# A written order for the sync queue, with stores between the last loads, and a new order of the steps in a retention and token-mixing kernel

## The chip, the cores and the metric

The kernel runs on one core of a Trainium2 chip. The time is the device time of the core in microseconds; the number compared is the median over runs. The profile is that of one execution, and its span runs from the first to the last instruction that the profiler recorded.

## What is computed

Two layers follow each other. The first is a retention recurrence over 768 tokens for 4 batches and 8 heads of 64:

```python
gamma = 1.0 - 2.0 ** (-5.0 - np.arange(H, dtype=np.float32))
for t in range(S):
    state = gamma[None, :, None, None] * state + np.einsum('bhd,bhe->bhde', k[:, :, t], v[:, :, t])
    y[:, :, t] = scale * np.einsum('bhd,bhde->bhe', q[:, :, t], state)
```

Its output is laid out as x, 768 tokens by 512 features in each batch. The second layer mixes tokens with weights that it makes from x, applies a relu, and projects:

```python
wq = x @ w_q
wk = x @ w_k
W_tok = scale * np.einsum('bsd,btd->bst', wq, wk)
mixed = np.einsum('bst,btd->bsd', W_tok, x)
return (np.maximum(mixed, 0.0) @ w_out).astype(np.float32)
```

Inputs and output are float32. q, k and v have 6.3 MB each, the output 6.3 MB.

## The kernel before

**Tiles.** The tokens of a batch are cut into three pairs of chunks of 128 tokens, twelve pairs in all (0 to 11). Of each pair, k, q and v are loaded whole, 512 KB each. The kernel computes in bf16 into PSUM, which is used as eight numbered banks.

**Steps.** Every piece of work is a named step with a pair, mostly a half or chunk, an engine (A for ScalarE, V for VectorE, P for GpSimd) and a PSUM bank. The list `ORDER` writes all steps down in one sequence, and a loop at the end of the kernel issues them as listed; there is no scheduler behind it, and each engine runs its own steps in the sequence of the list. For a pair p the steps are:
- `ck.p.c`, `cq.p`, `cv.p.c`: cast k and q from the loaded tile to bf16; scale and cast v (ck and cv are two instructions each). In the profile of before a cast on ScalarE is under L133, one on VectorE or GpSimd under L134, cv under L307.
- `trk`, `trq`: eight transposes each on TensorE (L335, L350); `ekT`, `eqT` copy the results out of PSUM.
- `sc.p.half`: products of q and k (L370); `eat`: masks them (L382). `st.p.c`: adds to the running state (L424); `es` copies it out. `in` and `ia`: the two parts of y, from the state (L410) and from the masked products (L444). `ex`: scales y into x (L458).
- `xt`, `exT`: transposes x (L474). `wqk`: x times w_q and w_k (L488), with `ewq` and `ew` copying out; `tw` and `ewt`: the transposed wq (L514). `zm.b`, `ez`: wk-transposed times x, summed over the three pairs of a batch (L536). `mx`: z times wq (L556); `r`: the relu (L571, L573).
- `pj.p.j`: the projection with w_out, four matmuls for each half j (L578); `eo.p.j`: copies the half into the output tile.
- `W` and `WO` cast the weights. `fill.n` issues n matmuls on zeros (L283), whose results nobody reads.

**Buffers.** Loaded tiles share a pool of 18 buffers: a load may be issued when the tile 18 places ahead of it has been cast. Bf16 k, q and v have three buffers each, transposed k and q two, the relu two, output tiles ten. A bank is written again only after its last reader.

**The sync queue.** SyncE issues all transfers but half of the first k, in program order; each instruction waits for its own semaphores, and those behind it wait too. `LOADS` gives the sequence of the loads (k, q, v with their pair, `w` for w_q and w_k, `o` for w_out). `more_loads` issues them as far as the buffers allow, and is called again when a tile has been cast. Stores are collected in `eo`: a pair is stored when both halves are evicted, pair 11 by halves. They are issued only when the list of loads is empty, in the sequence of their evictions:

```python
        if p == NG - 1:
            stores.append((p, j))
        elif outs[p] == 2:
            stores.append((p, None))
        if not queue:
            while stores:
                store(*stores.pop(0))
```

Loads are under L152 in the profile, stores under L609 (pair) and L611 (half).

Of the kernel before, what the change touches and what calls it, by code (L numbers as in the profile page):

```python
# [13 lines left out]


ORDER = """
ck.0.1:A cq.0.1:V ck.0.0:P fill.20@6 trk.0@6 cq.0.0:A ekT.0:V fill.1@0 trq.0@0 eqT.0:A fill.4@0
sc.0.1@0 ck.1.0:P sc.0.0@2 cv.0.0:V ck.1.1:A cq.1:A cv.0.1:P ck.2.1:P st.0.0 eat.0.1:V cv.1.1:P
fill.3@6 trk.1@6 fill.3@0 trq.1@0 eat.0.0:V ekT.1:A cv.2.0:P ia.0.1@2 ck.3.1:P es.0.0:V cv.1.0:V
st.0.1 in.0.1@2 ia.0.0@2 eqT.1:A sc.1.1@0 ck.2.0:A cv.2.1:P sc.1.0@4 ex.0:V es.0.1:A cq.2:A  # L20
fill.1@6 xt.0@6 st.1.0 eat.1.1:V es.1.0:A in.1.0@2 eat.1.0:V trk.2@0 ekT.2:V trq.2@1 exT.0:A
eqT.2:V ck.3.0:A ia.1.1@2 in.1.1@2 ia.1.0@2 fill.1@0 sc.2.0@0 st.1.1 ex.1:V es.1.1:A fill.2@6
xt.1@6 cv.3.0:P in.2.0@2 sc.2.1@4 st.2.0 eat.2.0:V trk.3@0 cq.3:A eat.2.1:V trq.3@1 es.2.0:A
in.2.1@2 exT.1:A eqT.3:A ia.2.1@2 ia.2.0@2 ekT.3:V ex.2:V fill.2@0 sc.3.0@0 sc.3.1@4 ck.4.0:P
eat.3.0:V eat.3.1:V cv.3.1:P st.3.0 W:A cv.4.0:P wqk.0@6 ck.4.1:A es.3.0:A xt.2@2 cq.4:A trk.4@3
wqk.1@0 ew.1:A ewq.1:A in.3.1@4 ewq.0:A trq.4@1 ia.3.1@4 cv.4.1:P ia.3.0@4 eqT.4:A ck.5.0:P
exT.2:V st.3.1 es.3.1:A ew.0:V wqk.2@6 ekT.4:V sc.4.1@0 tw.0@3 st.4.0 ew.2:A ewq.2:A ex.3:V
ewt.0:A eat.4.1:V cv.5.0:P sc.4.0@4 tw.1@6 tw.2@3 eat.4.0:V zm.0@2 es.4.0:A WO:P xt.3@0 ez.0:V
cq.5:A exT.3:V ewt.2:A trq.5@1 ck.5.1:A ewt.1:V ia.4.1@4 in.4.1@4 in.4.0@4 st.4.1 ia.4.0@4
wqk.3@6 es.4.1:V ck.6.0:P eqT.5:A ewq.3:A mx.2@2 trk.5@1 ex.4:V st.5.0 r.2:A xt.4@0 tw.3@2  # L30
ew.3:A ewt.3:A mx.1@4 es.5.0:A ekT.5:V r.1:A cv.5.1:P sc.5.0@2 exT.4:V eat.5.0:V sc.5.1@0
ck.6.1:A eat.5.1:V wqk.4@6 pj.2.0@4 ew.4:A pj.2.1@5 cv.6.0:P trk.6@0 cq.6:A eo.2.1:V ekT.6:V
ck.7.1:P eo.2.0:A trq.6@1 mx.0@4 eqT.6:V ewq.4:A r.0:A in.5.1@2 ck.7.0:A in.5.0@2 ia.5.1@2
ia.5.0@2 pj.1.0@6 sc.6.0@4 eo.1.0:A cv.6.1:P sc.6.1@0 ex.5:V cq.7:A st.6.0 xt.5@2 eat.6.0:V
exT.5:A cv.7.0:P pj.0.1@6 ck.8.0:P trk.7@4 eat.6.1:V cv.7.1:P es.6.0:V trq.7@5 wqk.5@2 ia.6.0@0
ekT.7:A ia.6.1@0 eqT.7:V ewq.5:V in.6.1@0 st.6.1 sc.7.1@4 ew.5:A eo.0.1:A ex.6:V sc.7.0@2
eat.7.1:V zm.1@6 es.6.1:A ck.8.1:A ez.1:A st.7.0 tw.5@0 cq.8:A eat.7.0:V ewt.5:A pj.1.1@1
trk.8@6 trq.8@4 eo.1.1:A ekT.8:V tw.4@5 es.7.0:A eqT.8:V ewt.4:A in.7.0@2 mx.5@0 in.7.1@2
ia.7.1@2 cv.8.0:P ia.7.0@2 r.5:A pj.0.0@6 ck.9.0:A cq.9:P ex.7:V eo.0.0:A st.7.1 sc.8.0@0
sc.8.1@4 es.7.1:V mx.4@2 st.8.0 eat.8.0:V pj.5.0@6 ck.9.1:A eat.8.1:V es.8.0:A xt.6@0 eo.5.0:A  # L40
cv.8.1:P xt.7@1 r.4:A trq.9@6 ck.10.0:A exT.6:V ck.10.1:P trk.9@4 ia.8.0@2 exT.7:V cv.9.0:P
ekT.9:A eqT.9:V cv.9.1:P wqk.6@0 ew.6:A wqk.7@1 trk.10@6 ia.8.1@2 in.8.1@2 in.8.0@2 ewq.6:V
ewq.7:A ew.7:V ekT.10:V ex.8:V sc.9.1@4 eat.9.1:V sc.9.0@0 cq.10:A st.9.0 ck.11.1:P pj.4.0@6
pj.5.1@2 es.9.0:A eat.9.0:V xt.8@3 eo.4.0:A trq.10@6 exT.8:V st.9.1 eo.5.1:A mx.3@4 eqT.10:V
ck.11.0:A in.9.1@0 cq.11:P ia.9.0@0 tw.6@2 r.3:A ia.9.1@0 ewt.6:A wqk.8@3 ex.9:V trk.11@6
trq.11@2 sc.10.1@4 cv.10.0:P ew.8:A es.9.1:A ewq.8:A tw.8@3 pj.3.0@0 ekT.11:V xt.9@6 eat.10.1:V
eqT.11:A ewt.8:A tw.7@1 sc.10.0@4 exT.9:V sc.11.1@2 eo.3.0:A ewt.7:A cv.10.1:P st.10.0 es.10.0:A
zm.2@1 st.10.1 es.10.1:A cv.11.0:P pj.4.1@6 ez.2:A st.11.0 eat.11.1:V eat.10.0:V sc.11.0@0
mx.8@2 es.11.0:A in.10.1@4 cv.11.1:P eat.11.0:V eo.4.1:A in.10.0@4 ia.10.1@4 ia.10.0@4 pj.3.1@6
ia.11.1@0 r.8:A in.11.1@0 ex.10:V mx.7@2 in.11.0@0 mx.6@4 eo.3.1:A ia.11.0@0 pj.8.0@6 ex.11:V  # L50
r.7:A wqk.9@2 xt.10@3 ewq.9:A ew.9:V pj.7.1@0 xt.11@2 exT.10:V wqk.10@3 ewq.10:A eo.8.0:V
exT.11:V eo.7.1:V pj.8.1@6 wqk.11@2 ew.10:V r.6:V ewq.11:A tw.9@3 pj.7.0@0 eo.8.1:V tw.11@1
ew.11:A ewt.11:A zm.3@2 eo.7.0:A ez.3:V pj.6.0@6 ewt.9:V tw.10@3 mx.9@0 mx.11@4 eo.6.0:A
ewt.10:V r.9:A mx.10@2 pj.6.1@6 pj.9.1@0 r.10:V pj.9.0@1 eo.6.1:A r.11:A pj.10.1@6 eo.10.1:A
pj.10.0@2 pj.11.1@6 eo.9.0:V pj.11.0@1 eo.11.1:A eo.10.0:V eo.11.0:A eo.9.1:V
""".split()


LOADS = "q0 v0 k1 q1 v1 k2 q2 v2 k3 q3 v3 w k4 q4 v4 k5 q5 v5 o k6 q6 v6 k7 q7 v7 k8 q8 v8 k9 q9 v9 k10 q10 v10 k11 q11 v11".split()

STAGES = 18
OBUFS = 10
# [3 lines left out]
def kernel(  # L66
# [15 lines left out]
    nc = tc.nc  # L82
# [7 lines left out]
    NG = B * NP  # L90
# [36 lines left out]
    pairs = [dict() for _ in range(NG)]  # L127
# [3 lines left out]
    def copy(e, out, in_):  # L131
        if e == "A":
            return nc.scalar.copy(out=out, in_=in_)  # L133
        return ENGINES[e].tensor_copy(out=out, in_=in_)  # L134
# [10 lines left out]
    def load(name, p, half=None, eng=None):  # L145
        src = {"k": k, "q": q, "v": v}[name]
        b, cp = divmod(p, NP)
        st = pairs[p]
        if name + "_st" not in st:
            st[name + "_st"] = stage_pool.tile([128, 2, HP, 2, D], FP32, name=name + "_st", tag="st")  # L150
        xs = slice(0, 2) if half is None else slice(half, half + 1)
        dma = (eng or nc.sync).dma_start(  # L152
            out=st[name + "_st"][:, xs].rearrange("g x hp j d -> g (x hp) (j d)"),
            in_=src[b, xs.start * HP : xs.stop * HP, cp * 2 * C : (cp + 1) * 2 * C, :].rearrange(
                "h (g j) d -> g h (j d)", j=2
            ),
        )
    def load_token(token):
        if token == "w":
            nc.sync.dma_start(out=wq_stage, in_=moe_w_q.rearrange("(a p) h -> p a h", p=128))  # L160
            nc.sync.dma_start(out=wk_stage, in_=moe_w_k.rearrange("(a p) h -> p a h", p=128))
        elif token == "o":
            for a in range(NDM):
                nc.sync.dma_start(
                    out=wout_stage[:, a], in_=moe_w_out[128 * a : 128 * a + 128, :], max_dma_last_dim=512
                )
        else:
            name, _, half = token[1:].partition("/")
            load(token[0], int(name), int(half) if half else None)

    load("k", 0, 0, nc.scalar)
    load("k", 0, 1, nc.sync)

    queue = list(LOADS)
    staged = ["k0"]
    cast = set()


    def more_loads():
        while queue:  # L180
            token, _, half = queue[0].partition("/")
            if token not in "wo" and token not in staged:
                n = len(staged)
                if n >= STAGES and staged[n - STAGES] not in cast:
                    return
                staged.append(token)
            load_token(queue.pop(0))
# [3 lines left out]
    def release(token, n):  # L191
        parts[token] = parts.get(token, 0) + 1
        if parts[token] == n:
            cast.add(token)
            more_loads()

    more_loads()


# [384 lines left out]
            )  # L584
        st["o_ps", j] = bank32(b)

    outs = {}

    def eo(e, b, p, j):
        st = pairs[p]  # L590
        if "o" not in st:
            st["o"] = ost_pool.tile([128, 2, DM], FP32, name="o_st")
        copy(e, st["o"][:, j], st["o_ps", j])
        outs[p] = outs.get(p, 0) + 1
        if p == NG - 1:
            stores.append((p, j))
        elif outs[p] == 2:
            stores.append((p, None))
        if not queue:
            while stores:  # L600
                store(*stores.pop(0))

    stores = []

    def store(p, j):
        b, cp = divmod(p, NP)
        dst = out[b, cp * 2 * C : (cp + 1) * 2 * C, :].rearrange("(g j) m -> g j m", j=2)
        if j is None:
            nc.sync.dma_start(out=dst, in_=pairs[p]["o"], max_dma_last_dim=512)  # L609
        else:  # L610
            nc.sync.dma_start(out=dst[:, j], in_=pairs[p]["o"][:, j], max_dma_last_dim=512)  # L611

    steps = dict(
        ck=ck, cq=cq, cv=cv, trk=trk, ekT=ekT, trq=trq, eqT=eqT, sc=sc, eat=eat, st=state,
        es=es, ia=ia, **{"in": inter}, ex=ex, xt=xt, exT=exT, wqk=wqk, ewq=ewq, ew=ew, tw=tw, ewt=ewt, zm=zm, ez=ez, mx=mx, r=r,
        pj=pj, eo=eo,
    )

    for token in ORDER:
        token, _, b = token.partition("@")  # L620
        token, _, e = token.partition(":")
# [38 lines left out]
```

## Time and profile before

| | |
|---|---|
| median of 9 runs | 103.4 us (102.22 to 104.27) |
| the profiled execution | 103.23 us, span 101.3 us |
| granted TensorE clock, mean | 0.979 |
| TensorE, VectorE busy | 87.1 us, 72.9 us |
| ScalarE, GpSimd busy | 71.7 us, 67.1 us |
| read from HBM, written to it | 20.19 MB, 6.29 MB |
| last load issued, landed | 62.59 us, 68.99 us |
| last store issued, landed | 96.27 us, 100.47 us |

Busy times overlap, and busy TensorE is not TensorE at its peak, since matmuls are pipelined. In the lines of the profile PE is TensorE, DVE VectorE, ACT ScalarE, POOL GpSimd, and SPq the queue of SyncE. A timeline line has start, duration, engine, line of the code, operation and tiles; a line of the chain has start, duration and what the last instruction was waiting for at that time. A row by stretch has the stretch and its length, then each engine's busy time with its instructions in brackets, then the granted clock, the busy share of the 16 transfer engines and what they moved.

### The profile page before, as it was taken

How to read it: one execution, taken by the hardware profiler on the slowest of the kernel's cores; microseconds unless marked ns; L12 is line 12 of the kernel's file. 1: busy time of each engine (PE TensorE's matmuls, PEld its weight loads, DVE VectorE, ACT ScalarE, POOL GpSimd, SP SyncE). 2: the span in 40 equal slices, each digit the busy share in tenths (PEclk: the TensorE clock that was granted, in tenths of full speed). 3: DMA queues.
4: the chain of work that ended last, by engine and by line, in shares of the span. 5: the costliest groups of instructions: out<-in, count | busy, mean ns of one | idle time of the engine just before them, and what ended most of it. 6: DMA issues, size and time to landing. Idle time of an engine off the chain costs nothing.

```text
span 101.3 us, 3245 instructions
## 1 busy us (share of the span) xinstructions
PE 87.1 (86%) x1341; PEld 59.7 (59%) x1341; DVE 72.9 (72%) x108; ACT 71.7 (71%) x125; POOL 67.1 (66%) x86
## 2 busy tenths in 40 slices
PE   5995996999688799989998989999999999999300
PEld 1343674767576587566875669659667776544100
DVE  3017599998949958879999795699898689445200
ACT  4275798789697599889899999959947614645400
POOL 6542969999899997999999999999998000000000
PEclk9999999999999999999999999999999999999965
DMA  1999999999999999999999999999921930686395
GB/s 24 292 347 347 347 347 344 298 267 265 289 283 324 262 287 304 313 280 330 328 320 317 300 277 329 340 335 334 347 89 32 298 91 0 190 244 190 106 346 169
DMA packets 53134, 26.68 MB, mean 263 GB/s; under 512 B 1920, under 2 KB 53120, under 8 KB 53120
## 3 DMA queue, kind: packets, MB, share of 16 engines
q1 hardware_dynamic: 52592, 26.22, 87.4%
q10 hardware_dynamic: 528, 0.26, 0.9%
q8 instruction: 10, 0.16, 0.6%
q14 instruction: 4, 0.03, 0.1%
HBM read 20.19 MB, written 6.29 MB: 261 GB/s over the span
## 4 chain that ended last, share of the span: by engine, by line
PE 38%; POOL 16%; DMA 13%; ACT 9%; SPq 7%; DVE 6%; issue 4%; ACTq 0%; DVEq 0%; POOLq 0%
PE banks L578 15%; POOL vs L307 12%; DMA q_st<-in_q_dram 7%; SPq L152 7%; DMA k_st<-in_k_dram 6%; POOL ks L134 4%; DVE at_sb L382 3%; PE banks L444 3%; ACT ks L133 3%; PE banks L488 3%; PE banks L350 3%; PE banks L370 3%; PE banks L474 2%; PE banks L556 2%; PE banks L424 2%
## 5 line engine op out<-in xcount | busy, mean ns | idle before, releaser
L307 POOL TENSOR_TENSOR vs<-v_st,fv 64x512 bf16<-64x512 f32 x44 | 45.9, 1044 | 3.0 <-DMA v_st<-in_v_dram 0.2
L382 DVE TENSOR_TENSOR at_sb<-banks,cmask 128x1024 bf16<-128x1024 f32 x24 | 28.4, 1217 | 2.3 <-POOL ks L134 1.2
L578 PE MATMUL banks<-wout_sb,relu 128*128 128x512 bf16 x96 | 23.6, 379 | 0.2
L133 ACT CAST ks<-k_st 64x512 bf16<-64x512 f32 x26 | 16.0, 616 | 4.0 <-DMA k_st<-in_k_dram 3.7
L134 POOL CAST ks<-k_st 64x512 bf16<-64x512 f32 x22 | 14.2, 645 | 6.2 <-DMA k_st<-in_k_dram 4.9
L458 DVE TENSOR_TENSOR x_nat<-banks,fy 128x1024 bf16<-128x1024 f32 x12 | 14.7, 1221 | 2.4 <-PE banks L444 2.1
L578 PEld LDWEIGHTS <-relu 128*128 128x128 bf16 x96 | 8.5, 97 | 8.7 <-issue 1.0
L283 PE MATMUL banks<-warm 128*128 128x512 bf16 x37 | 11.3, 438 | 2.4 <-DVE warm L202 1.3
L133 ACT COPY o_st<-banks 128x512 f32<-128x512 f32 x17 | 10.0, 586 | 4.3 <-PE banks L578 4.1
L571 ACT ACTIVATE relu<-banks 128x1024 bf16<-128x1024 f32 x10 | 10.3, 1031 | 1.7 <-PE banks L578 1.2
L133 ACT CAST qs<-q_st 128x1024 bf16<-128x1024 f32 (+1 forms) x10 | 10.1, 1006 | 1.8 <-DMA q_st<-in_q_dram 1.6
L444 PE MATMUL banks<-vs,at_sb 128*128 128x64 bf16 x192 | 8.8, 194 | 0.2 <-POOL vs L307 0.2
L370 PE MATMUL banks<-qT,kT 64*128 64x128 bf16 x192 | 8.3, 218 | 0.6 <-DVE wqn L134 0.2
L350 PE MATMUL banks<-identity,qs 128*128 128x128 bf16 x96 | 7.3, 220 | 1.7 <-ACT qs L133 1.4
L133 ACT CAST s_sb<-banks 128x256 bf16<-128x256 f32 x16 | 6.0, 377 | 3.2 <-PE banks L424 3.0
L474 PE MATMUL banks<-identity,x_nat 128*128 128x128 bf16 x96 | 7.2, 220 | 0.9 <-DVE x_nat L458 0.9
L444 PEld LDWEIGHTS <-at_sb 128*128 128x128 bf16 x192 | 7.2, 98 | 1.1 <-issue 0.5
L335 PE MATMUL banks<-identity,ks 128*128 128x128 bf16 x96 | 7.4, 220 | 0.4 <-POOL ks L134 0.4
L370 PEld LDWEIGHTS <-kT 64*128 64x128 bf16 x192 | 5.9, 94 | 3.1 <-issue 2.4
L350 PEld LDWEIGHTS <-qs 128*128 128x128 bf16 x96 | 5.9, 98 | 2.9 <-ACT qs L133 2.1
L283 PEld LDWEIGHTS <-warm 128*128 128x128 bf16 x37 | 3.7, 110 | 6.6 <-issue 3.6
L474 PEld LDWEIGHTS <-x_nat 128*128 128x128 bf16 x96 | 5.8, 98 | 2.9 <-DVE x_nat L458 1.7
(59 smaller groups left out, 120.6 us busy)
## 6 DMA issues: line engine op xcount, KB each, us to landing
q_st<-in_q_dram SPq DMA_DIRECT2D x12, 512.0 KB, 6.3
v_st<-in_v_dram SPq DMA_DIRECT2D x12, 512.0 KB, 6.5
k_st<-in_k_dram SPq DMA_DIRECT2D x11, 512.0 KB, 6.5
out_dram<-o_st SPq DMA_DIRECT2D x11, 512.0 KB, 4.2
wout_stage<-in_moe_w_out_dram SPq DMA_DIRECT2D x4, 256.0 KB, 5.0
out_dram<-o_st SPq DMA_DIRECT2D x2, 256.0 KB, 2.9
k_st<-in_k_dram ACTq DMA_DIRECT2D x1, 256.0 KB, 4.2
k_st<-in_k_dram SPq DMA_DIRECT2D x1, 256.0 KB, 3.8
```

What stands on the lines that cost most here:

```text
L133: return nc.scalar.copy(out=out, in_=in_)
L134: return ENGINES[e].tensor_copy(out=out, in_=in_)
L283: nc.tensor.matmul(out=bank32(b), lhsT=warm[:, 0:128], rhs=warm, start=True, stop=True)
L307: ENGINES[e].tensor_tensor(out=st["vs"][rows(j), c].rearrange("p hp x d -> p x hp d"), in0=st["v_st"][rows(c), :, :, j], in1=fv[rows(c), p ...
L350: nc.tensor.transpose(ps[:, hp, :, j, :], st["qs"][:, hp, j].rearrange("p x d -> p (x d)"), identity,)
L370: nc.tensor.matmul(out=ps[:, x, hi, c, :], lhsT=st["kT"][rows(x), hp, c, :], rhs=st["qT"][rows(x), hp, c, :], start=(hi == 0 and c == 0), ...
L382: ENGINES[e].tensor_tensor(out=st["at", half].rearrange("p x hi c t -> p (x hi c) t"), in0=st["at_ps", half].rearrange("p (n t) -> p n t", ...
L444: nc.tensor.matmul(out=y[:, x, c, hp, :], lhsT=st["at", half][:, x, hi, c, :], rhs=st["vs"][:, c, hp, x, :], start=first(p, x), stop=False ...
L458: nc.vector.tensor_tensor(out=st["x"].rearrange("p x c i n -> p (x c i n)").rearrange("p (m d) -> p m d", d=D), in0=st["y_ps"].rearrange(" ...
L474: nc.tensor.transpose(ps[:, a, c, :], st["x"][:, a // 2, c, a % 2, :], identity)
L571: nc.scalar.activation(out=dst, in_=st["mx_ps"], func=ACT.Relu)
L578: nc.tensor.matmul(out=bank32(b), lhsT=st["relu"][:, a, j, :], rhs=wout_sb[:, a, :], start=(a == 0), stop=(a == NDM - 1),)
```

## The change

The list of the sync queue now holds stores as well, `s` with the pair, or with pair and half. `more_loads` stops at a store until its halves have been evicted, issues it, and goes on. The evictions call `more_loads` where they kept a list of their own. Up to q10 the loads keep their sequence; s0 then comes ahead of v10, s1 behind k11, s2 behind q11, and the remaining stores behind v11.

`ORDER` is written anew as a whole: the same steps (apart from six `fill` steps with 28 matmuls in place of nine with 37), in another sequence, partly on other engines and banks. Steps per engine that differ:

| step | before (A, V, P) | after (A, V, P) |
|---|---|---|
| ck | 13, 0, 11 | 15, 2, 7 |
| cq | 10, 1, 2 | 8, 1, 4 |
| cv | 0, 2, 22 | 0, 1, 23 |
| ekT | 3, 9, 0 | 5, 7, 0 |
| exT | 3, 9, 0 | 6, 6, 0 |
| es | 16, 4, 0 | 13, 7, 0 |
| ewq | 10, 2, 0 | 8, 4, 0 |
| ewt | 9, 3, 0 | 6, 6, 0 |
| r | 10, 2, 0 | 9, 3, 0 |

GpSimd's list in the new order, from pair 5 on: cv.5.0, cv.5.1, WO, cq.6, cv.6.0, cv.6.1, ck.7.1, cv.7.0, cv.7.1, cv.8.1, cv.8.0, ck.9.1, cq.9, ck.10.0, cq.10, cv.9.0, cv.9.1, ck.11.0, cq.11, cv.10.0, cv.10.1, cv.11.0, cv.11.1. Before, WO stood ahead of ck.6.0 and cv.5.1, and the end of the list was cq.9, cv.8.1, ck.10.1, cv.9.0, cv.9.1, ck.11.1, cq.11, cv.10.0, cv.10.1, cv.11.0, cv.11.1.

The core of the diff, with the last rows of both orders:

```diff
-ew.11:A ewt.11:A zm.3@2 eo.7.0:A ez.3:V pj.6.0@6 ewt.9:V tw.10@3 mx.9@0 mx.11@4 eo.6.0:A
-ewt.10:V r.9:A mx.10@2 pj.6.1@6 pj.9.1@0 r.10:V pj.9.0@1 eo.6.1:A r.11:A pj.10.1@6 eo.10.1:A
-pj.10.0@2 pj.11.1@6 eo.9.0:V pj.11.0@1 eo.11.1:A eo.10.0:V eo.11.0:A eo.9.1:V
...
+ewq.10:V eo.7.1:A wqk.11@3 ew.11:A tw.9@6 pj.7.0@2 ewq.11:A tw.10@3 ewt.10:V zm.3@4 ewt.9:A
+pj.8.0@6 ez.3:V tw.11@3 eo.7.0:A eo.8.0:A mx.10@4 mx.9@0 ewt.11:V mx.11@2 pj.8.1@6 r.10:A
+pj.10.1@4 r.11:V pj.10.0@5 eo.10.1:V pj.11.1@2 pj.11.0@4 eo.8.1:A eo.10.0:A r.9:V pj.9.0@6
+eo.9.0:A pj.9.1@5 eo.11.0:V eo.9.1:A eo.11.1:V
...
-LOADS = "q0 v0 k1 q1 v1 k2 q2 v2 k3 q3 v3 w k4 q4 v4 k5 q5 v5 o k6 q6 v6 k7 q7 v7 k8 q8 v8 k9 q9 v9 k10 q10 v10 k11 q11 v11".split()
+LOADS = """
+q0 v0 k1 q1 v1 k2 q2 v2 k3 q3 v3 w k4 q4 v4 k5 q5 v5 o k6 q6 v6 k7 q7 v7 k8 q8 v8 k9 q9 v9 k10
+q10 s0 v10 k11 s1 q11 s2 v11 s4 s3 s5 s6 s7 s8 s10 s11/0 s11/1 s9
+""".split()
...
     def more_loads():
         while queue:
-            token, _, half = queue[0].partition("/")
-            if token not in "wo" and token not in staged:
+            token = queue[0]
+            if token[0] == "s":
+                if not stored(token[1:]):
+                    return
+                queue.pop(0)
+                continue
+            if token not in "wo":
...
         copy(e, st["o"][:, j], st["o_ps", j])
-        outs[p] = outs.get(p, 0) + 1
-        if p == NG - 1:
-            stores.append((p, j))
-        elif outs[p] == 2:
-            stores.append((p, None))
-        if not queue:
-            while stores:
-                store(*stores.pop(0))
+        evicted.add((p, j))
+        more_loads()
...
+    def stored(name):
+        p, _, j = name.partition("/")
+        p, js = int(p), [int(j)] if j else [0, 1]
+        if not all((p, i) in evicted for i in js):
+            return False
         b, cp = divmod(p, NP)
         dst = out[b, cp * 2 * C : (cp + 1) * 2 * C, :].rearrange("(g j) m -> g j m", j=2)
-        if j is None:
-            nc.sync.dma_start(out=dst, in_=pairs[p]["o"], max_dma_last_dim=512)
-        else:
-            nc.sync.dma_start(out=dst[:, j], in_=pairs[p]["o"][:, j], max_dma_last_dim=512)
+        src = pairs[p]["o"]
+        if j:
+            dst, src = dst[:, int(j)], src[:, int(j)]
+        nc.sync.dma_start(out=dst, in_=src, max_dma_last_dim=512)
+        return True
```

## Prediction

> **What bounds the kernel now.** I read the slices of the page first, then busy time by stretch, then the chain that ended last, then the timelines of POOL and of the sync queue.
>
> ```profile
> PE   5995996999688799989998989999999999999300
> DMA  1999999999999999999999999999921930686395
> GB/s 24 292 347 347 347 347 344 298 267 265 289 283 324 262 287 304 313 280 330 328 320 317 300 277 329 340 335 334 347 89 32 298 91 0 190 244 190 106 346 169
> ```
>
> Transfers are busy to about 73 us, nearly idle afterwards, and full again in the next to last slice (346 GB/s), when PE has already stopped.
>
> ```profile
> core 0: us, PE busy (x) PEld busy (x) DVE busy (x) ACT busy (x) POOL busy (x), PEclk, DMA share, GB/s
> 8.00:44.00 36.00, 30.89 (x553) 22.86 (x552) 30.96 (x37) 29.61 (x50) 30.76 (x33) 1.00 1.04 305
> 44.00:66.00 22.00, 21.07 (x395) 15.79 (x393) 18.31 (x24) 20.79 (x36) 20.45 (x24) 1.00 1.06 313
> 66.00:95.00 29.00, 28.44 (x371) 18.07 (x368) 22.27 (x29) 17.51 (x34) 11.56 (x12) 1.00 0.62 186
> 95.00:101.30 6.30, 0.00 (x0) 0.00 (x0) 0.00 (x0) 0.33 (x1) 0.00 (x0) 0.66 0.83 250
> ```
>
> From 44 us PE is never long without work; from 66 us it is the bound; behind 95 us only stores are left. The chain agrees:
>
> ```profile
> 73.84 1.04 POOL vs L307
> 74.88 0.06 issue
> 74.94 1.05 POOL vs L307
> ...
> 88.48 6.23 PE banks L578 x28
> 94.72 0.02 issue
> 94.74 0.58 ACT o_st L133
> ```
>
> So the time is two terms: when the last projection ends (94.72) and what follows it (101.3 - 94.72 = 6.6 us). The sync queue shows why the second is so long:
>
> ```profile
> 62.59 1.78 SPq L152 DMA_DIRECT2D v_st<-in_v_dram  x1
> 64.47 26.00 SPq L609 DMA_DIRECT2D out_dram<-o_st  x9
> 94.49 0.37 SPq L611 DMA_DIRECT2D out_dram<-o_st  x1
> 94.96 0.45 SPq L609 DMA_DIRECT2D out_dram<-o_st  x1
> 95.50 0.67 SPq L611 DMA_DIRECT2D out_dram<-o_st  x1
> 96.27 0.68 SPq L609 DMA_DIRECT2D out_dram<-o_st  x1
> ```
>
> All loads precede all stores, and the last four stores, 256 + 512 + 256 + 512 KB, are issued within 1.8 us. In the trace the last lands at 100.47, 4.2 us behind its issue.
>
> **The tail.** The new last steps are pj.10.1, 10.0, 11.1, 11.0, 9.0, 9.1, with stores s10, s11/0, s11/1, s9. Let X be the end of pj.9.1. A projection takes PE 0.865 us, an eviction 0.6 with its handoff on either engine. Pair 10 is evicted at X - 2.9 and its 512 KB are out by about X + 0.2; s11/0 can start at X - 1, s11/1 at X - 0.3; s9 at X + 0.7, when at most 256 KB are ahead of it. Stores of 512 KB with little in front landed 2.9 to 3.0 us after issue (77.33 to 80.25, 79.21 to 82.14, 90.10 to 93.05), so s9 lands at X + 3.7, and the span ends 0.85 later as before: X + 4.5, 2.1 less than 6.6. If s9 is still met by a backlog and takes the 4.2 of before, the gain is 0.8. The Trainium skill ("DMA: Bandwidth & Descriptors", Latency and other measured facts) speaks of a fixed cost near 2 us; with 1.5 us of transfer (512 KB at 347 GB/s) that is 3.5 and a gain of 1.5. The rows show 1.4 us besides the transfer; I take 2.1, and 0.8 for the range.
> The relu buffers (two) and banks hold up here by margins I count by hand: r.11 must wait for pj.8.1 (X - 5.2), then eo.10.1, then r.9 done at X - 2.0, and pj.9.0 starts at X - 1.7. A DVE that is 0.3 us later moves the end.
>
> **Stores among the loads.** s0, s1, s2 are put ahead of v10, q11 and v11 (s1 behind k11). Each is a 512 KB transfer; in the mixed stretch of before, stores landed 1.5 us apart (71.26, 72.70, 74.21, 75.72), as loads do (64.28, 65.77, 67.32, 68.99). So v10 lands at 65.8, k11 at 67.3, q11 at 70.3, v11 at 73.5. The queue also waits for the evictions now, with everything behind them: s0 needs eo.0.1, at about 52; s1 needs eo.1.1, at 57; s2 needs eo.2.1, at 58.5. SP reaches them only at 62.6, 65.5 and 68, so these waits cost nothing while the evictions keep 5 us in hand.
> Who waits for the late loads? POOL's order. It scales v: a cv step is two instructions of 1.04 us, 2.2 with gaps; a ck 1.3; a cq 1.07. With v6 at 44.15 its row runs: cv.6 to 48.6, ck.7.1 49.9, cv.7 and cv.8 58.7, ck.9.1 60.0, cq.9 61.1, ck.10.0 62.4, cq.10 (q10 lands at 62.6) 63.7, cv.9 68.1, ck.11.0 69.4, cq.11 (q11 at 70.3) 71.4, cv.10 and cv.11 to 80.2. The row of before ended at 78.20:
>
> ```profile
> 67.05 1.26 POOL L134 CAST ks<-k_st 64x512 bf16<-64x512 f32 x2
> 68.38 1.03 POOL L134 CAST qs<-q_st 128x1024 bf16<-128x1024 f32 x1
> 69.38 8.82 POOL L307 TENSOR_TENSOR vs<-v_st,fv 64x512 bf16<-64x512 f32 x8
> ```
>
> So the last v is 2 us later. On ACT ck.11.1 waits for k11 (67.3), with eo.4.1, r.5, exT.7 and eqT.11 behind it; exT.7 is then done at 70.9, and PE wants it at 71.2.
>
> **The order of PE.** Removed: 9 of 37 filler matmuls, 0.216 us each, 1.9 us, all before 33 us, where PE waits for data anyway: nothing. The page on the clock ("TensorE: Matmul & The Clock Gate", What's actually happening) speaks against it: an idle window of 3.4 us halves the clock. Before, a gap of 1.1 us at 8.6 us left the clock at 1.00; the longest I work out in the new start is about as long. If it did fall, 3.4 us at half clock lose 1.7 us, against a cushion there of over 5 us (below). I take nothing.
> For the rest I take start-to-start times from the dense part of the PE timeline: a group of 8 transposes 0.46, of q.k 0.28, of the state 0.245, intra-chunk 0.285, inter-chunk 0.17, wqk 0.46, z 0.78, mx 0.23, a projection 0.865. For each step I add what PE still has from it on; start plus remainder is the earliest end. Before, it is 85.9 at trk.2, 90.2 at trq.5, 91.7 at trq.6 (43.79 + 47.9), 93.0 at trq.9, 94.1 at trq.11, 94.4 at st.11.0 (76.03): each rise is PE time lost.
> In the new order I put each step at the first moment that its loads, casts and buffers allow. trk.2 at 16.1 with 68.3 left: 84.4. trk.5 at 34.2 with 56.0: 90.2. w_out's cast now follows cv.5.1 on POOL, done at 41.9; pj.0.0 then has 50.2 left: 92.2; trq.6 at 43.85 with 48.4: 92.2 as well. trk.7 needs ck.7.1, which POOL does behind cv.6.1, 49.95 with 43.3: 93.25. st.8.0 needs cv.8.0, which now follows cv.8.1, 58.9 with 34.7: 93.6. st.9.0 waits for cv.9.0 (65.9), behind cq.10, 66.0 with 28.4: 94.4. trk.11 waits for ck.11.0, 69.45 with 25.4: 94.85. From there the gates hold without a new rise: st.11.0 at 79.2 (cv.11.0 at 78.0), ia.11.1 at 80.5 with 14.3 left (cv.11.1 at 80.2). So X = 94.85 by what I can name, 0.1 above 94.72. Handoffs that I can't name can only add; before, gaps over 0.15 us in the PE timeline from 44 to 94 sum to 1.0 us. Bounds 0 and 1.0; I add 0.5, since about half of such gaps are gates counted already.
>
> **Engines of the evictions and casts.** ck: ACT 13 to 15, POOL 11 to 7, DVE none to 2; cv on POOL 22 to 23; cq on POOL 2 to 4; two copies of transposed k and three of transposed x move from DVE (0.60) to ACT (0.91), and small copies (es, ewq, ewt) from ACT to DVE. By these prices ACT has 68.5 us in place of 66.5, DVE 70.0 for 69.5, POOL 66.0 for 67.0: none above PE's 72 of real work, and what matters of their order is in the gates above. A ck on DVE isn't in the trace: below by its q cast of the same 512 columns, 0.43, two make 0.9; above by POOL's 1.3. I take 0.9; both lie before 11 us, under the cushion.
>
> **The sum.** Tail -2.1, PE +0.1 and +0.5: 101.3 - 1.5 = 99.8 for a profiled execution. That one took 103.23 with 101.3 of span, 1.9 us around it, and lies 0.2 under the median of 103.4; 103.4 - 1.5 = 101.9.
>
> **Rivals.** First, the order buys PE time as well: if the named gates are not reached because POOL or transfers run a little ahead (0.5 us at trk.11) X is 94.2, and the time 101.9 - 1.1 = 100.8. For it: up to 40 us the new gates are no higher than those of before (90.2 at trq.5 in both); against: POOL's row is 2 us later at its end.
> Second, no visible change: the tail gains only 0.8 and small handoffs cost the whole 1.0: 103.4 - 0.8 + 1.1 = 103.7. For it: many steps have margins of 0.3 us; against: the lone stores' landing rows.
> Third, slower: a store among the loads costs them more than its own 1.5 us. q11 has two stores ahead, and cq.11 stands in front of four cv steps on POOL, which can't overtake it: q11 + 9.9 us is the end of cv.11.1, and PE has 14.3 us left from there. At 3.0 us for each store q11 lands at 73.3, cv.11.1 ends at 83.2, X = 97.6 + 0.5 and the time is 103.4 + 3.4 - 2.1 = 104.7. It decides from about 2.9 us a store, or if s1's eviction comes after about 67 us instead of 57. Against it: the even 1.5 us of mixed landings.
>
> **How the numbers follow.** Likeliest case 0.48, PE gain 0.14, no visible change 0.24, slower 0.14. A measurement here can tell about 1% from no change, so faster is below 102.4 and slower above 104.4. Faster holds the likeliest case less a part that slips over the bound, and the first rival: 0.55; within 1%: 0.31; slower 0.14. The likeliest case alone has 101.2 to 102.8. The range reaches from the first rival's 100.8 to the edge of the third: 100.8 to 104.5.
>
> **What would show it.** Right: 4 to 5 us between the last projection and the end, the last store landing about 3 us after its issue, v10, k11, q11, v11 1.5 to 4.5 us later than before, cv.11.1 ending near 80 on POOL, the last projection ending at 94.5 to 95.8. Wrong: POOL or ACT idle before its last casts for a late k11 or q11 by more than 1 us; PE gaps over 0.5 us behind 70 us; a granted clock below 1.00 before 30 us; the last store landing 4 us after its issue.

## The result, and the profile after

| | before | after |
|---|---|---|
| median | 102.7 us (36 runs; the first nine, shown above, gave 103.4) | 100.83 us (11 runs, 100.19 to 104.73) |
| ratio of the times | 1 | 0.979, 95% interval 0.975 to 0.983 |
| profiled execution | 103.23 us, span 101.3 | 100.19 us, span 98.5 |
| last projection ends | 94.72 | 94.10 |
| from there to the end of the span | 6.60 | 4.38 |
| granted clock, mean | 0.979 | 0.959 |

The kernel became faster by 2.1%. Some executions of most of these kernels take 1.5 to 6.5 us longer than its fastest; the ratios leave them out and the medians don't, so the two needn't agree. Below, X is the end of the last projection, and the tail is what the span has behind it.

The slices of the page after, clock, busy share of the transfer engines and bandwidth:

```profile
PEclk9999955799999999999999999999999999999997
DMA  1999999999999999999999979999977600772995
GB/s 25 281 346 347 347 347 344 339 290 261 305 298 272 328 336 338 343 336 333 316 277 323 332 218 330 298 340 325 304 227 228 208 5 7 213 213 83 317 290 166
```

Two things are to be seen. The transfers at the end are spread wider: the last three slices hold 317, 290 and 166 GB/s, where before they had 106, 346 and 169. And the clock drops to 5 to 7 tenths in slices 6 to 8 (12.3 to 19.7 us), which it did not do before; by the trace it was halved from 11.87 to 18.70 us. The same by stretch, with the columns of the table that the prediction shows:

```profile
8.00:44.00 36.00, 31.42 (x569) 23.95 (x567) 32.36 (x39) 30.72 (x52) 31.16 (x30) 0.91 1.09 321
44.00:66.00 22.00, 21.16 (x364) 15.40 (x362) 18.64 (x23) 20.89 (x36) 19.51 (x23) 1.00 1.05 308
66.00:95.00 29.00, 28.02 (x376) 17.68 (x374) 21.64 (x32) 18.65 (x32) 11.39 (x12) 1.00 0.67 199
95.00:98.50 3.50, 0.00 (x0) 0.00 (x0) 0.00 (x0) 0.00 (x0) 0.00 (x0) 0.82 0.69 209
```

PE has the same dense work from 44 us on (21.2 of 22 us), and only 3.5 us follow behind 95 us instead of 6.3. The chain ends as before, 0.6 us earlier:

```profile
87.94 6.16 PE banks L587 x28
94.10 0.02 issue
94.12 0.58 ACT o_st L137
```

The sync queue's timeline, where the stores (L616) come between the last loads (L156), and the last four stores:

```profile
56.93 1.31 SPq L616 DMA_DIRECT2D out_dram<-o_st  x1
58.29 1.44 SPq L156 DMA_DIRECT2D v_st<-in_v_dram  x1
59.82 1.34 SPq L156 DMA_DIRECT2D k_st<-in_k_dram  x1
61.26 2.10 SPq L616 DMA_DIRECT2D out_dram<-o_st  x1
63.41 1.36 SPq L156 DMA_DIRECT2D q_st<-in_q_dram  x1
64.87 1.39 SPq L616 DMA_DIRECT2D out_dram<-o_st  x1
66.31 1.44 SPq L156 DMA_DIRECT2D v_st<-in_v_dram  x1
...
91.28 0.37 SPq L616 DMA_DIRECT2D out_dram<-o_st  x1
93.11 0.37 SPq L616 DMA_DIRECT2D out_dram<-o_st  x1
93.71 0.37 SPq L616 DMA_DIRECT2D out_dram<-o_st  x1
94.73 0.37 SPq L616 DMA_DIRECT2D out_dram<-o_st  x1
```

In the first group every line takes 1.3 to 2.1 us, and no store waits for its eviction: those of pairs 0, 1 and 2 were over at 51.0, 56.7 and 58.1. They landed in turn at 62.8 (s0), 64.8 (v10), 66.3 (k11), 67.8 (s1), 69.3 (q11), 70.8 (s2) and 73.3 (v11). From q10 (61.3) to v11 it took 12.0 us where it took 6.4 before, so the three stores cost the loads behind them 5.6 us, 1.9 each, of which 1.5 is a transfer's own time. The last four stores are issued over 3.5 us where it was 1.8; the last landed at 97.64, 2.9 us behind its issue.

### The profile page after: what moved, and what is told of

It reads as the page before. It is cut to its first block, busy times and chain, and to the rows that moved or that the text cites. A ratio compares the mean times of both kernels' runs of the same rounds, so it can differ in the third digit from the quotient of the medians.

```text
span 98.5 us, 3221 instructions
## 1 busy us (share of the span) xinstructions
PE 87.3 (89%) x1332; PEld 60.0 (61%) x1332; DVE 75.2 (76%) x114; ACT 72.5 (74%) x123; POOL 66.8 (68%) x82
## 4 chain that ended last, share of the span: by engine, by line
PE 47%; DVE 19%; ACT 17%; DMA 6%; issue 5%; SPq 1%; DVEq 0%; ACTq 0%
PE banks L587 18%; DVE at_sb L391 9%; DMA v_st<-in_v_dram 6%; ACT ks L137 6%; PE banks L453 6%; DVE x_nat L467 4%; PE banks L497 3%; PE banks L419 3%; PE banks L379 3%; ACT o_st L137 3%; PE banks L359 2%; PE banks L483 2%; DVE vs L316 2%; PE banks L565 2%; DVE kT L138 2%
## 5 line engine op out<-in xcount | busy, mean ns | idle before, releaser
L316 POOL TENSOR_TENSOR vs<-v_st,fv 64x512 bf16<-64x512 f32 x46 | 48.9, 1062 | 7.3 <-DMA v_st<-in_v_dram 4.7
L137 ACT CAST ks<-k_st 64x512 bf16<-64x512 f32 x30 | 18.6, 619 | 1.2 <-DMA k_st<-in_k_dram 0.9
L292 PE MATMUL banks<-warm 128*128 128x512 bf16 x28 | 9.5, 485 | 2.0 <-DVE warm L211 1.3
L137 ACT CAST qs<-q_st 128x1024 bf16<-128x1024 f32 (+1 forms) x8 | 8.0, 996 | 3.5 <-DMA q_st<-in_q_dram 3.5
L138 POOL CAST ks<-k_st 64x512 bf16<-64x512 f32 x14 | 8.9, 634 | 2.4 <-ACT wk_n L137 1.0
L379 PE MATMUL banks<-qT,kT 64*128 64x128 bf16 x192 | 9.2, 225 | 1.2 <-DVE kT L138 0.9
L580 ACT ACTIVATE relu<-banks 128x1024 bf16<-128x1024 f32 x9 | 9.3, 1035 | 1.2 <-PE banks L565 1.2
L433 PE MATMUL banks<-vs,ks 128*64 128x64 bf16 x160 | 6.5, 206 | 1.8 <-DVE vs L316 1.8
L497 PE MATMUL banks<-wqk_w,xT 128*128 128x128 bf16 x96 | 7.4, 220 | 0.1
L137 ACT COPY xT<-banks 128x1024 bf16<-128x1024 bf16 x6 | 6.1, 1022 | 1.7 <-PE banks L483 1.6
```

The source lines that it names most:

```text
L292: nc.tensor.matmul(out=bank32(b), lhsT=warm[:, 0:128], rhs=warm, start=True, stop=True)
L316: ENGINES[e].tensor_tensor(out=st["vs"][rows(j), c].rearrange("p hp x d -> p x hp d"), in0=st["v_st"][rows(c), :, :, j], in1=fv[rows(c), p ...
L379: nc.tensor.matmul(out=ps[:, x, hi, c, :], lhsT=st["kT"][rows(x), hp, c, :], rhs=st["qT"][rows(x), hp, c, :], start=(hi == 0 and c == 0), ...
L497: nc.tensor.matmul(out=ps[:, c, :], lhsT=st["xT"][:, a, c, :], rhs=wqk_sb[:, a, :], start=(c == 0 and a == 0), stop=(a == NDM - 1), skip_g ...
```

## The experiments

Each ratio is against the kernel before on the same chip. In the expectations, T is the theory that the tail came from the sequence of the last evictions and stores, S that it came from the stores moved between the loads; C1 says that the fallen clock costs time at the end and C0 that it doesn't; P says that the stores between the loads have a price, N that they have none. What further letters stand for is said in the expectations themselves. All of these kernels compute the whole output; added `fill` steps multiply zeros that nobody reads.

**The base again.** No edit.

> The kernel before, once more. In its first profile q6 landed at 42.67 us, in the changed kernel's at 40.25, though the loads up to q6 are the same list. Theory L (the earlier loads are chance between executions): q6 of this profile lands anywhere from 40 to 43, and the last projection ends earlier by about what q6 is earlier; the span behind the last projection stays 6.6 +- 0.3 us. Theory O (the new order lets the loads go faster): q6 again at 42.4 to 42.9. Ratio to the kernel before 0.995 to 1.005 in both.

Measured: 0.998 (0.994 to 1.002), median 102.28 over 12 runs, beside 102.48 over 17 of the same kernel. So a typical time of the kernel before is 102.3 to 102.5, and the 103.4 that the prediction started from was about 1 us too high. q6 landed at 42.6 in this profile, which decides nothing between L and O.

**Stores behind the loads, all else as after.**

```diff
-q10 s0 v10 k11 s1 q11 s2 v11 s4 s3 s5 s6 s7 s8 s10 s11/0 s11/1 s9
+q10 v10 k11 q11 v11 s0 s1 s2 s4 s3 s5 s6 s7 s8 s10 s11/0 s11/1 s9
```

> The changed kernel with s0, s1, s2 moved behind v11, so that all loads precede all stores as before. Theory T (the gain is in the tail: the sequence of the last projections and stores): behind the last projection still 4.4 us, v11 lands 4 us earlier, cv.11.1 ends about 1.3 us earlier on POOL, the last projection at most 0.3 us earlier, since PE has work waiting; ratio 0.976 to 0.983, the changed kernel's own 0.979. Theory S (stores between the loads bring the gain, by leaving fewer transfers for the end): the tail grows by the 4.5 us of three stores less the idle time behind them, at least 1 us; ratio 0.99 or more.

Measured: 0.975 (0.968 to 0.982), not slower than the change itself; X 94.10, tail 4.40. S falls: with all stores behind all loads again the tail is as short. The last load landed at 68.3 instead of 73.3, and POOL's last casts came 1.1 us earlier:

```profile
68.39 1.03 POOL L138 CAST qs<-q_st 128x1024 bf16<-128x1024 f32 x1
69.39 8.82 POOL L316 TENSOR_TENSOR vs<-v_st,fv 64x512 bf16<-64x512 f32 x8
```

Yet X is the same: in the new order PE doesn't wait for them.

**The tail alone, in the kernel before.** One eviction of pair 9 is moved from the last place to where its projection is done, so that s9 goes out ahead of pairs 10 and 11.

```diff
-... r.11:A pj.10.1@6 eo.10.1:A
+... r.11:A eo.9.1:V pj.10.1@6 eo.10.1:A
...
-pj.10.0@2 pj.11.1@6 eo.9.0:V pj.11.0@1 eo.11.1:A eo.10.0:V eo.11.0:A eo.9.1:V
+pj.10.0@2 pj.11.1@6 eo.9.0:V pj.11.0@1 eo.11.1:A eo.10.0:V eo.11.0:A
```

> The kernel before with one step moved: the eviction of pair 9's second half (eo.9.1) no longer comes last on VectorE but right behind the relu of pair 10; so the store of pair 9 leaves ahead of the last three. Theory T: the last store is then 256 KB, which landed at 99.02 in the profile of before when it was third of the four; the end comes 1.45 us earlier, 5.1 us behind the last projection, ratio 0.983 to 0.989. Theory O (the new order of the steps as a whole is what gains, on PE): no change, 0.996 to 1.004.

Measured: 0.985 (0.979 to 0.990), or -1.6 us of 102.5, and a tail of 5.1 in place of 6.6. Its chain and its last stores:

```profile
88.98 6.23 PE banks L578 x28
95.22 0.02 issue
95.24 0.58 ACT o_st L133
```

```profile
94.99 0.37 SPq L611 DMA_DIRECT2D out_dram<-o_st  x1
95.45 0.46 SPq L609 DMA_DIRECT2D out_dram<-o_st  x1
96.00 0.68 SPq L611 DMA_DIRECT2D out_dram<-o_st  x1
```

Of the four stores of before, one 512 KB store has left the end, and the span ends 1.5 us nearer to the last projection: 512 KB at 347 GB/s. (The profile is of an execution of 102.3 us, so its X of 95.2 says nothing beside the others.) T holds, and one moved eviction gives most of what the whole change gave.

**More fillers at the start.** Ten filler matmuls are put where PE waited.

```diff
-ck.0.1:V cq.0.0:A ck.0.0:P fill.20@6 trk.0@6 cq.0.1:V trq.0@0 cv.0.0:V ekT.0:A eqT.0:A st.0.0
-... fill.1@6 trk.1@6
+ck.0.1:V cq.0.0:A ck.0.0:P fill.20@6 trk.0@6 cq.0.1:V trq.0@0 fill.7@4 cv.0.0:V ekT.0:A eqT.0:A st.0.0
+... fill.1@6 trk.1@6 fill.3@4
```

> The changed kernel with ten filler matmuls more, seven behind trq.0 and three behind trk.1, on a bank not yet in use. In its profile the granted clock fell to about half from 12.9 to 18 us, behind a PE gap of 1.8 us. Theory C0 (the cushion of the start covers it): the clock stays at 1.00 there and the time doesn't change, ratio 0.976 to 0.983. Theory C1 (the lost 2.5 us of clock reach the end): 0.5 to 1.5 us faster than the changed kernel, ratio 0.965 to 0.974.

Measured: 0.969 (0.962 to 0.975), X 92.97, tail 4.40. First the kernel after, by stretch, then two lines of its PE, of which the first shows how long PE stood still and for whom:

```profile
8.00:13.00 5.00, 2.52 (x42) 1.91 (x40) 4.78 (x5) 4.76 (x7) 3.37 (x3) 0.89 1.15 347
13.00:20.00 7.00, 6.74 (x89) 5.00 (x89) 4.68 (x6) 3.80 (x7) 6.57 (x8) 0.59 1.14 340
```

```profile
10.32 0.32 PE L433 MATMUL banks<-vs,ks 128*64 128x64 bf16 x8 [1.83 <-DVE vs L316]
14.44 1.06 PE L359 MATMUL banks<-identity,qs 128*128 128x128 bf16 x8
```

Then the same with the fillers:

```profile
8.00:13.00 5.00, 4.08 (x46) 2.15 (x44) 4.91 (x6) 4.88 (x7) 3.54 (x3) 1.00 1.15 347
13.00:20.00 7.00, 5.59 (x115) 4.38 (x114) 6.33 (x7) 4.50 (x8) 6.57 (x8) 1.00 1.13 337
```

```profile
10.11 0.32 PE L433 MATMUL banks<-vs,ks 128*64 128x64 bf16 x8 [0.50 <-DVE vs L316]
13.64 0.61 PE L359 MATMUL banks<-identity,qs 128*128 128x128 bf16 x8
```

In the profile after, PE was busy for 2.5 of the 5 us up to 13, the clock went to 0.59, and eight transposes took 1.06 us instead of 0.61: 89 matmuls got done from 13 to 20 us, against 115. By start plus remainder trk.2 is at 86.85 after and at 84.46 with fillers, trk.4 at 89.5 and 88.2, trk.5 at 90.2 and 89.2, X at 94.10 and 92.97. Between these two profiles about half of the start's loss, 1.1 of 2.4 us, is still there at the end. The runs below have to say whether that is more than the scatter of X.

**After again.** No edit; on one chip with the next three kernels.

> The changed kernel once more, on one chip with the three kernels beside it. Theory C1 (the clock's fall at 13 to 18 us costs about 1 us): the clock falls again behind the gap at 8.5 us, PE's start plus remainder at trk.5 is again about 90.2, ratio 0.977 to 0.984. Theory C0 (the filler matmuls gained by the chance of loads): this kernel is as fast as the one with ten filler matmuls more, 0.967 to 0.974.

Measured: 0.986 (0.981 to 0.991), median 101.08; X 94.6, tail 4.4. The clock fell again, for half as long (12.99 to 16.40 us; mean 0.76 from 13 to 20). Here the change is worth 1.4 us.

**Fillers, and the last store by halves.** To the fillers this adds:

```diff
-... s10 s11/0 s11/1 s9
+... s10 s11/0 s11/1 s9/0 s9/1
```

> The changed kernel with the ten filler matmuls and with pair 9 stored by halves (s11/0, s11/1, s9/0, s9/1), so that only 256 KB leave behind the last projection. 256 KB landed 2.3 us after issue where 512 KB took 2.9: the tail falls from 4.4 to 3.8 us. Theory T (the tail is what follows the last eviction): 0.6 us under the kernel with the filler matmuls alone, ratio 0.960 to 0.967. Rival (the last landing is bound by the queue's backlog of 1 MB, not by its own size): no change, 0.967 to 0.972.

Measured: 0.977 (0.971 to 0.984), X 94.97, tail 4.44. The halves gained nothing. Its last half was issued at 95.68, 0.7 us behind X, and took 2.8 us to land although it has only 256 KB: from 95 to 98 us the transfers ran at 338 to 346 GB/s, about 1 MB of stores. The tail of the new order is bounded by what is still to be written at X, not by the last store's own latency.

**The written queue alone.** The kernel before with the new `more_loads`, three stores between the loads as in the change (s2, s1, s0, since they are evicted so there), and the rest in the sequence of its own evictions:

```diff
+q10 s2 v10 k11 s1 q11 s0 v11 s5 s4 s3 s8 s7 s6 s11/1 s10 s11/0 s9
```

> The old order of the steps with the new sync queue: s2, s1, s0 between the last loads in the sequence of their evictions there, all later stores in their old sequence. Theory T (the gain is in the sequence at the end): the tail stays 6.6 us, the last loads land 1.5 to 4.5 us later, POOL's row ends up to 2 us later and the last projection by 0 to 1 us; ratio 0.998 to 1.010. Theory S (stores between the loads gain): 0.985 to 0.992. In its profile, Theory L (early loads are chance) has q6 land between 40 and 43 whatever the order; Theory O has it at 42.4 to 42.9 as in all profiles of the old order so far.

Measured: 1.0075 (1.003 to 1.012), with a median of 104.7 us over all twelve executions, of which six took 105.4 to 109.3 us; why these six took so long was not found. X 95.08, tail 6.6. In the old order the stores between the loads do cost. Its POOL and PE:

```profile
68.74 1.04 POOL L138 CAST qs<-q_st 128x1024 bf16<-128x1024 f32 x1 [1.72 <-DMA q_st<-in_q_dram]
69.74 8.83 POOL L316 TENSOR_TENSOR vs<-v_st,fv 64x512 bf16<-64x512 f32 x8
```

```profile
74.18 0.32 PE L433 MATMUL banks<-vs,ks 128*64 128x64 bf16 x8 [0.30 <-POOL vs L316]
76.39 0.32 PE L433 MATMUL banks<-vs,ks 128*64 128x64 bf16 x8 [0.93 <-POOL vs L316]
```

POOL stands 1.7 us for q11 behind two stores, the eight cv instructions follow, and PE waits 0.3 and 0.9 us for v: start plus remainder rises from 93.2 at trq.11 to 94.8 at st.11.0. That is the mechanism of the prediction's slower rival, at 1.9 us a store instead of its 3 (from the landing of q10 to that of q11 it took 8.6 us, 4.7 before). In the new order POOL waits for q11 as well:

```profile
66.88 1.25 POOL L138 CAST ks<-k_st 64x512 bf16<-64x512 f32 x2
69.45 1.03 POOL L138 CAST qs<-q_st 128x1024 bf16<-128x1024 f32 x1 [1.32 <-DMA q_st<-in_q_dram]
70.45 8.82 POOL L316 TENSOR_TENSOR vs<-v_st,fv 64x512 bf16<-64x512 f32 x8
```

Behind 66 us PE shows no wait for POOL in that order, though: it comes to cv's results late enough.

This kernel also had q6 landed at 40.3 us, as early as after the change, with the old order of the steps: an early q6 is not a property of the new order.

**Fewer fillers in the kernel before.** Four filler steps with eleven matmuls are taken out (the change has nine fewer).

```diff
-... ekT.0:V fill.1@0 trq.0@0 eqT.0:A fill.4@0
-fill.3@6 trk.1@6 fill.3@0 trq.1@0 ...
+... ekT.0:V trq.0@0 eqT.0:A
+trk.1@6 trq.1@0 ...
```

> The kernel before without eleven of its filler matmuls, those between trk.0 and trq.1. Theory C1 (a fall of the clock at the start reaches the end): the clock falls to about half near 10 to 18 us and the time rises by 0.5 to 1.5 us, ratio 1.005 to 1.015. Theory C0 (the cushion of the start covers it): the clock falls and the time stays, 0.996 to 1.004. If the clock doesn't fall, nothing is told.

Measured: 1.001 (0.998 to 1.005); in its profile X 93.85, tail 6.6, q6 landed at 41.8, and the clock stayed at 1.00. It didn't in all executions. Each has a mean granted clock; the tail alone, with an idle PE, brings it to about 0.98 in the old order, and below 0.97 it has probably fallen at the start too, though no profile of this kernel shows it. With the bound at 0.967, which was set when the means were known:

| kernel | executions with the clock at 0.967 or less |
|---|---|
| before (its own runs and those beside the others) | 2 of 62 |
| the written queue alone, with all fillers | 4 of 12, each of 105.5 us or more |
| fewer fillers | 7 of 12 |
| after | 12 of 25 |
| stores behind the loads, without more fillers | 5 of 12 |
| more fillers, in four variants | 0 of 24 |

So fillers guard the clock, and removing them is enough to let it fall about every second time. (Whether it fell at the start in the four executions of the second row isn't known.) The traces show more closely when it falls. In all profiles the clock changes in steps of 3.41 us: each stretch of one clock but the last is a whole multiple of that, 6.83 us for the fall after the change and 3.41 us in the run after again. Here are the last 3.41 us before the fall after the change, the fall, and the emptiest such stretch of the profile with fewer fillers:

```profile
8.46:11.87 3.41, 1.45 (x30) 1.10 (x29) 3.35 (x4) 3.37 (x6) 2.66 (x2) 1.00 1.15 347
11.87:18.70 6.83, 6.10 (x73) 4.32 (x74) 4.48 (x6) 4.26 (x7) 5.75 (x7) 0.50 1.15 345
9.51:12.92 3.41, 2.03 (x40) 1.67 (x40) 3.37 (x4) 3.35 (x5) 3.23 (x4) 1.00 1.15 347
```

PE was busy for 1.45 of 3.41 us, or 42%, and the clock fell; with 2.03, or 59%, it stayed. In the five profiles with a fall it was 41 to 56%, in the nine others the emptiest stretch of the first 20 us (once PE works) had 59 to 74%. The limit between 56 and 59% is an estimate from these fourteen. The longest gap doesn't tell: after again the clock fell with none over 1.03 us, and with fewer fillers it stayed behind one of 1.10. Where the stretches begin differs from one execution to the next, which may be why the same kernel lets the clock fall in one and not in another.

What a fall costs is another matter. Of the kernel with fewer fillers the seven have a mean of 102.5 us and the five others 102.4. Of the executions of the kernel after that its ratios count, five with a fallen clock have 101.1 and ten others 100.8, with spreads of 1.5 and 1.2 us. The bound separates them badly: the profile after again, with its shorter fall, has a mean clock of 0.979 and is among the ten.

The time being that of the kernel before, this profile (102.27 us) also shows a typical execution of the old order:

```profile
87.61 6.23 PE banks L578 x28
93.84 0.02 issue
93.87 0.59 ACT o_st L133
```

**Fillers and stores once more, all on one chip.** After unchanged; after with the stores behind the loads; with the fillers; with both.

> One of four kernels on one chip: stores between the last loads or behind them, with or without ten filler matmuls more. This one is the changed kernel: between, without. Both theories: ratio 0.978 to 0.988, 4.4 us behind the last projection.

> Stores behind all loads, without the filler matmuls. Theory N (the stores between the loads cost and gain nothing, since POOL ends just in time for PE): within 0.3% of the changed kernel beside it. Theory P (they delay POOL's last casts, as the old order's did, and cost): 0.4 to 1.0% faster than it.

> Stores between the loads, with the filler matmuls. Theory C1 (the fall of the clock at the start reaches the end): 0.6 to 1.3% faster than the changed kernel beside it. Theory C0 (it does not): within 0.4% of it, and the gain on the other chip was the chance of the loads.

> Stores behind all loads, with the filler matmuls. The two effects add: under N and C0 within 0.4% of the changed kernel, under P and C1 1.0 to 2.3% faster, and the fastest of all.

| kernel | ratio | 95% interval |
|---|---|---|
| after | 0.987 | 0.977 to 0.997 |
| stores behind the loads | 0.980 | 0.973 to 0.987 |
| fillers | 0.979 | 0.972 to 0.985 |
| both | 0.978 | 0.972 to 0.984 |

The intervals overlap, and the first row rests on two executions (the others on four, four and six), so this comparison separates neither C0 from C1 nor N from P, and the two edits don't add up. Kernels with fillers came out at 0.969 (against 0.979, not on one chip), 0.977 against 0.986 (with the halves) and 0.979 against 0.987: each time 0.8 to 1.0% less, none beyond its interval; with the stores behind the loads they brought 0.2% (0.978 against 0.980). X in their profiles is 92.97, 94.97, 94.4 and 93.5, after the change 94.10 and 94.6, so X doesn't tell them apart either. The gates do for the first half: trk.2 is at 84.4 to 84.5 with fillers and at 85.9 to 86.9 in three profiles without (after, after again, stores behind the loads), trk.5 at 88.7 to 89.7 and at 89.7 to 90.3. Behind that the order is lost, trk.11 at 92.6 to 94.5 and at 93.6 to 93.8: in the run with the halves, for one, the loads landed some 2 us later from v7 on (48.9, with fillers alone 46.6). A gain of the fillers of some tenths of a us up to 1 us is likely; that the clock's loss reaches the end isn't shown, since executions of one kernel with and without the fall, as far as the mean clock tells them apart, differ by 0.3 us at most. The version with both edits has the best median of this chip, 100.09 us, all six executions between 99.57 and 100.83.

## Why the prediction was about right in its gain and wrong in its time

**The tail: right.** Predicted 6.6 to 4.5 us, measured 4.38; -2.1 against -2.2. The cause holds too: the tail is the sequence of the last evictions. Moving it alone gave 1.5 us, leaving it alone in the new queue kept 6.6, and the new order without the moved stores kept 4.4. Of the two prices weighed for s9, the rows' 2.9 to 3.0 us and the 3.5 us by the page, the rows held: 2.9. That is in part luck. The prediction had at most 256 KB ahead of s9; at its issue both halves of pair 11 were still under way (they landed at 95.4 and 96.1), and by halves it was no faster, since a backlog of 1 MB ends at about the same time. The latency of a lone store is not the only bound there.

**The stores among the loads: right in place, too cheap, without a gain.** "Each is a 512 KB transfer" at 1.5 us: the landings came at 64.8, 66.3, 69.3 and 73.3 where 65.8, 67.3, 70.3 and 73.5 were worked out, and cv.11.1 ended at 79.3 (80.2). The agreement is partly luck: q10 had landed at 61.3 instead of 62.6, and the three stores cost 1.9 us each. No run shows a gain from them: without them the change has 0.975 and 0.980, with them 0.979 to 0.987. In the old order they cost 0.75%, by the slower rival's path.

**PE: right as a difference, wrong as a place.** Predicted was +0.6 on X. Against the typical old execution of the run with fewer fillers (93.85) X came at 94.10 and 94.6, so +0.25 and +0.75. The ratios agree: gains of 2.2, 1.4 and 1.3 us with 2.2 off the tail leave 0 to 0.9 us for PE.

**The base: wrong.** The step that failed is the last of the sum, "That one took 103.23 with 101.3 of span, 1.9 us around it, and lies 0.2 under the median of 103.4; 103.4 - 1.5 = 101.9". One profiled execution and nine runs were taken for the kernel. The later runs of it have medians of 102.3 to 102.7. With 102.7 the sum gives 101.2; measured 100.83, and on two other sets 1.3 and 1.4 us below the kernel before. The gain of 1.5 lies among what the three ratios show (2.2, 1.4 and 1.3 us), though below the interval of the first, 1.7 to 2.6 us. The range hung on the same base: its lower end of 100.8, set against 103.4, is 0.9 us too high for a base of 102.5.

The gates stood on that one execution as well. Its q6 landed at 42.67; in the profiles read here since it landed at 41.8 and 40.3 in the old order and at 40.2 to 41.1 in the new; it was late again in two executions of the old order (103.8 and 102.3 us; 42.6 and 42.7) and two of the new (103.9 and 102.9 us; 42.1 and 41.7). "trq.6 at 43.85 with 48.4: 92.2" was measured at 91.6, and behind it trk.7 at 91.9 for 93.25, st.8.0 at 93.4 for 93.6, st.9.0 at 93.4 for 94.4, trk.11 at 93.7 for 94.85. That is how X was put at 95.35 where 94.10 was measured. Why the same list of loads lands up to 2 us apart was not found.

**The start: the step on gaps and clock failed too, its price at the end is open.** "I take nothing", with "the longest I work out in the new start is about as long" as 1.1 us. It was 1.83 us, with 0.64 us more at 12.5. What was mis-sized are three durations on DVE and POOL, which both work on float32 tiles there. First cv.0.0 of before, then the kernel after:

```profile
8.60 1.37 DVE L307 TENSOR_TENSOR vs<-v_st,fv 64x512 bf16<-64x512 f32 x2
```

```profile
8.13 2.14 DVE L316 TENSOR_TENSOR vs<-v_st,fv 64x512 bf16<-64x512 f32 x2 [1.20 <-DMA v_st<-in_v_dram]
10.30 1.60 DVE L138 CAST ks<-k_st 64x512 bf16<-64x512 f32 x2
```

```profile
8.18 3.00 POOL L316 TENSOR_TENSOR vs<-v_st,fv 64x512 bf16<-64x512 f32 x2 [1.53 <-DMA v_st<-in_v_dram]
```

cv.0.0 took 2.14 us on DVE (1.37 before, when POOL began a microsecond later), the ck 1.60 (0.9 was taken, 1.3 the upper bound), and cv.0.1 on POOL 3.00 where the pair has 2.2. Taken one by one, four instructions in turn are longer by what was left of the other engine's instruction when they began, less 0.13 us: 0.51 us for 0.64 left, 0.77 for 0.90, 0.36 for 0.49, 0.74 for 0.88 (undisturbed they take 1.04, 0.67, 1.04 and 0.42). That is the picture of two engines taking turns. st.0.0 waits for cv.0.0, and PE for it.

The Trainium skill ("TensorE: Matmul & The Clock Gate", What's actually happening) lets the clock fall behind an idle window of about 3.4 us; the steps of 3.41 us in the traces agree with that length, but the window need not be idle throughout: PE busy for 1.45 us of it, or for 1.91 after again, was not enough to keep the clock. Its warning was right. To compare the longest gap with that of before was the wrong test: after again the gap was 1.03 us, as short as the prediction had it, and the clock fell all the same.

The gate of trk.2, worked out as 84.4, was at 86.85 after the change, at 85.87 after again with the shorter fall, and at 84.46 with fillers. So it came 2.4 and 1.4 us later than with fillers; the prediction's estimate from the page, 1.7 us lost in one window, was of the right size. Whether that costs time at the end is what the cushion "of over 5 us" decides. By the prediction's own gates it is 5.8 us, from trk.2 at 84.4 to trk.5 at 90.2. But the steps between them moved with the start: trk.4 came at 89.5 and with fillers at 88.2. That trk.5 came at 90.2 as predicted is luck, since that is its place with the fallen clock; with fillers it was at 88.7 to 89.7. Between executions of one kernel the fall seems to cost 0.3 us or less; between kernels, fillers bring 0.8 to 1.0% in three pairs and 0.2% in a fourth. So its price at the end may be anything up to 1 us. Two of the signs named for a wrong prediction, a clock below 1.00 before 30 us and POOL idle over 1 us for q11, were there, and the time was still below the likeliest case.

**The rivals.** The time, 100.83, is that of the first rival, and so is X, 94.10 for its 94.2; its condition came true as well, since the transfers ran ahead (v6 landed at 41.75 instead of 44.15). But they do so in the old order too (X 93.85), so PE gained nothing by the new one. "No visible change" fell with the tail. The slower one is real in the old order and hidden in the new, whose PE asks for v later.

## What to carry to other kernels

Before a prediction is put on a base, the base needs more than one profile: a landing that sets gates should be read from several executions, and the difference trusted before the time. At the end of a kernel that stores a large output, count what is still to be written when the last matmul ends, and put the last evictions so that the stores are spread ahead of it; that was the whole gain here. Where fillers are removed from a start, add up how long PE works in each stretch of some 3.4 us and not only its longest gap, expect the clock to fall in some executions, and work out the next gates before calling it free.

## What the runs showed of the hardware

- Eight transposes went from 0.61 to 1.06 us when the granted clock was halved. It changed in steps of 3.41 us and fell behind steps in which PE was busy 41 to 56%, the longest gaps being 1.03 to 2.00 us; with 59% and more it stayed, behind a gap of 1.10 us too. The same kernel let it fall in one execution and not in the next (mean clock 0.957 and 1.000 after the change).
- DVE and POOL slowed each other when both worked on float32 tiles: 3.00 instead of 2.15 us for two cv instructions on POOL, 2.14 instead of 1.37 on DVE. The single instructions look like taking turns, each waiting for what is left of the other's. The start alone shows this; no run measured it apart.
- At the end, with about 1 MB of stores still to be written, a last store of 256 KB landed 2.8 us behind its issue, one of 512 KB 2.9 us: the backlog, not the size of the last store, set the time.
